# Query weights turned by VectorE in 32x32 blocks and gathered by small transfers, in place of identity products

## The chip, the cores and the metric

The kernel runs on one core of one Trainium2 chip. The time is device microseconds of the whole launch; the kernel before took 2062.61 us (median of three runs, 2061.29 to 2062.94). A profile of one more execution comes with it, and all durations below are from that execution. Engines are written as in the profile: PE is TensorE's matmuls, PEld its weight loads, DVE is VectorE, ACT is ScalarE, POOL is GpSimd, and SP (SPq) is SyncE, the queue that issues every transfer of this kernel.

## The reference: what is computed

Two stages follow each other over 4 batches of 12480 tokens with 128 channels.

1. Agent attention. 49 agents per batch attend to all keys and gather the values (`agent_v`, 49x128). Every query then attends to the 49 agents, and its softmax weights (49 numbers per token) mix `agent_v`.
2. A feed-forward layer over all 49920 tokens: `max(x @ w_in, 0)` squared, times `w_out`, with 2048 hidden channels.

```python
a2k = sm(agents, k)
agent_v = a2k @ v
q2a = sm(q, agents)
x = q2a @ agent_v
h = np.maximum(x @ w_in, 0.0)
out = h * h @ w_out
```

All inputs and outputs are float32.

## The kernel before

**Folding.** The kernel never forms `x`. It folds `agent_v @ w_in` into one table per batch (`aw_hi`, 128 rows by 2048 hidden channels), and multiplies the query weights of a token (49 numbers) with it directly. To keep float32 precision with fp32r operands, both factors are split into a high and a low part. The operand `w` therefore stacks 128 rows: rows 0 to 48 are the high parts of the 49 weights, rows 49 to 97 the low parts, and rows 98 to 127 a copy of rows 0 to 29, which meets the low parts of the table there. The 19 high rows that no longer fit (30 to 48) are copied four times into a second operand `x`, one copy at the start of each 32-row group, for a short product with K = 19.

**Tiling.** Tokens are handled in 52 blocks of 960 (`BLK`), 13 per batch. A block has two halves of 480 tokens (`G`), and each half passes through 16 chunks of 128 hidden channels. The main loop counts *slots* `k`: a slot is one pair of chunks of one half, so a block has 16 slots, 0 to 7 for the first half (j = 0) and 8 to 15 for the second. Two slots are issued together. For each such pair PE has four long products with `w` (`first`, into `h`), four short ones with `x`, and twelve products of the second layer (`second`, into `o`), which lag four slots behind. ACT takes `relu` and the square's high part, DVE the product `r*h` and half of the low parts, POOL the other half of the low parts (L372). The column `L337` in the profile is the helper `queued`, which issues all of these in one fixed order per engine.

**Query weights.** `queries(g)` prepares the weights of block g while block g-1 runs. It is a generator, and the main loop lets it go one step in slot 0 and one step in each slot from 2 on. The steps before the change: load `qt` (L285); eight tiles of 120 tokens times the 49 agents (L290, PSUM tile `psa`); the maximum and the subtraction on DVE (L293, L295); `exp` on ACT (L297); the sum, its reciprocal and the scaling of `e` (L300 to L303, the last on POOL); the split into `pp` (120 tokens by 8 tiles by 98), high part on ACT (L188) and low part on POOL (L190). Here tokens lie on partitions, while `w` needs the 49 agents on partitions. So for each half PE multiplies four tiles of `pp` by a 120x120 identity (L312), ACT copies the 98x480 result into `w` (L317), and SP issues one copy for rows 98 to 127 of `w` (L320) and four for `x` (L322). `w` and `x` have two buffers for each half.

**Background.** In the first three batches, another generator prepares the keys, values and tables of the next batch in the same slots (`background`: lines 141 to 277 of the profile). The last batch has no such work. Before the main loop a preamble loads the weights and does batch 0 and the first block's query weights.

**What sets the order.** `queued` chains the main work of PE, ACT and DVE by hand. Everything else is put into the engines' streams by a planner when the program is built: it plays the program on a timeline with costs of its own, and an instruction that stands earlier in the program goes first among those that are ready. On the chip each engine, and SP, then runs its stream strictly in that order. An instruction that waits holds up all that stands behind it on its engine.

Of the kernel before, what the change touches and what calls it, by code (L numbers as in the profile page):

```python
# [9 lines left out]
F32 = mybir.dt.float32  # L10
F32R = mybir.dt.float32r
# [6 lines left out]
P = 128  # L18
TP = 120
NT = 8  # L20
BLK = TP * NT
G = BLK // 2
# [16 lines left out]
def agent_attention_relu2(ctx: ExitStack, tc: tile.TileContext, qT, kT, v, agT, w_in, w_out, outT):  # L39
    nc = tc.nc  # L40
    C, NTOK = qT.shape
    _, B, NA = agT.shape
    N = NTOK // B
# [4 lines left out]
    K2 = 2 * NA  # L48
    SP = P - K2
    NL = NA - SP  # L50
    NQ = P // 32
    scale = 1.0 / math.sqrt(C)

    const = ctx.enter_context(tc.tile_pool(name="const", bufs=1))
# [3 lines left out]
    aw = ctx.enter_context(tc.tile_pool(name="aw", bufs=2))  # L58
    qp = ctx.enter_context(tc.tile_pool(name="qp", bufs=2))
# [8 lines left out]
    nc.gpsimd.memset(ones, 1.0)  # L68
    ident = const.tile([P, P], F32, name="ident")
    make_identity(nc, ident)  # L70
    identr = const.tile([TP, TP], F32R, name="identr")
    nc.scalar.copy(identr, ident[:TP, :TP])

    quad = const.tile([K2, 2, NA], F32, name="quad")
    nc.gpsimd.tensor_copy(quad, ident[:K2, :K2].rearrange("p (h a) -> p h a", h=2))
# [50 lines left out]
    last = {}  # L126
# [3 lines left out]
    def bank():  # L130
        if alone[0]:
            return ps_h.tile([P, 2, 512], F32, name="h")[:, 0, :]
        return ps_a.tile([P, 512], F32, name="psa")
# [51 lines left out]
    def halves(out, x, n, eng):  # L185

        w = x.shape[2]
        nc.scalar.copy(out[:, :, :w], x)  # L188
        yield
        last[eng] = eng.tensor_sub(out[:, :, n : n + w], x, out[:, :, :w].bitcast(F32))  # L190
# [52 lines left out]
    def tables(b):  # L243
        st = state[b]
        qd = quad.rearrange("p h a -> p (h a)")
        if "x" not in st:
            st["x"] = small.tile([K2, C + 1], F32, name="x")
            nc.vector.tensor_add(st["x"], st["av"][:, : C + 1], st["av"][:, C + 1 :])
        x = st["x"]
        yield  # L250
        pa = bank()
        nc.tensor.matmul(pa[:C, :K2], x[:, :C], qd, start=True, stop=True)
        nc.tensor.matmul(pa[:K2, K2 : K2 + 1], qd, x[:, C:], start=True, stop=True)
        yield
        av = small.tile([C, K2], F32, name="avT")
        nc.scalar.copy(av, pa[:C, :K2])
        rl = small.tile([K2, 1], F32, name="rl")
        nc.vector.tensor_scalar_add(rl, pa[:K2, K2 : K2 + 1], 1e-9)
        nc.vector.reciprocal(rl, rl)
        hi = st["hi"] = aw.tile([P, FF], F32R, name="aw_hi")  # L260
        ex = st["lo"] = aw.tile([P, NCH // NQ, P], F32R, name="aw_ex")
        for n in range(FF // 512):
            yield
            cs = slice(n * 512, (n + 1) * 512)
            pw = bank()
            nc.tensor.matmul(pw[:K2, :], av, win[:, cs], start=True, stop=True)  # L266
            yield
            last[nc.scalar] = nc.scalar.activation(hi[:K2, cs], pw[:K2, :], AF.Copy, scale=rl)
            lo = aw.tile([NA, 512], F32R, name="aw_lo", bufs=3)
            last[nc.vector] = nc.vector.scalar_tensor_tensor(  # L270
                out=lo, in0=pw[:NA, :], scalar=rl[:NA, :], in1=hi[:NA, cs].bitcast(F32),
                op0=ALU.mult, op1=ALU.subtract,
            )
            yield
            nc.sync.dma_start(hi[K2:, cs].bitcast(F32), lo[:SP, :].bitcast(F32))
            for t in range(NQ):
                nc.sync.dma_start(ex[t * 32 : t * 32 + NL, n, :].bitcast(F32), lo[SP:, t * P : (t + 1) * P].bitcast(F32))


    weights = {}  # L280

    def queries(g):
        b = g // NB
        qt = qp.tile([C, BLK], F32, name="qt", bufs=1)
        nc.sync.dma_start(qt, qT[:, g * BLK : (g + 1) * BLK])  # L285
        yield
        ps = bank()
        sv = ps[:TP, : NT * NA].rearrange("p (t a) -> p t a", a=NA)
        for t in range(NT):
            nc.tensor.matmul(sv[:, t, :], qt[:, t * TP : (t + 1) * TP], ag[:, b, :], start=True, stop=True)  # L290
        yield
        m = qp.tile([TP, NT, 1], F32, name="m", bufs=1)
        nc.vector.reduce_max(m, sv, axis=AX.X)  # L293
        e = qp.tile([TP, NT, NA], F32, name="e", bufs=1)
        nc.vector.tensor_sub(e, sv, m.broadcast_to([TP, NT, NA]))  # L295
        yield
        nc.scalar.activation(e, e, AF.Exp, scale=scale)  # L297
        yield
        z = qp.tile([TP, NT, 1], F32, name="z", bufs=1)
        nc.vector.reduce_sum(z, e, axis=AX.X)  # L300
        nc.vector.tensor_scalar_add(z, z, 1e-9)  # L301
        nc.vector.reciprocal(z, z)
        nc.gpsimd.tensor_mul(e, e, z.broadcast_to([TP, NT, NA]))  # L303
        yield
        pp = qp.tile([TP, NT, K2], F32R, name="pp", bufs=1)
        yield from halves(pp, e, NA, nc.gpsimd)
        weights[g] = []
        for j in range(2):
            yield
            pt = bank()  # L310
            for t in range(NT // 2):
                nc.tensor.matmul(  # L312
                    pt[:K2, t * TP : (t + 1) * TP], pp[:, j * (NT // 2) + t, :], identr, start=True, stop=True
                )
            w = qp.tile([P, G], F32R, name=f"w{j}", bufs=2)
            x = qp.tile([P, G], F32R, name=f"x{j}", bufs=2)
            nc.scalar.copy(w[:K2, :], pt[:K2, :G])  # L317
            weights[g].append((w, x))
            yield
            nc.sync.dma_start(w[K2:, :].bitcast(F32), w[:SP, :].bitcast(F32))  # L320
            for t in range(NQ):
                nc.sync.dma_start(x[t * 32 : t * 32 + NL, :].bitcast(F32), w[SP:NA, :].bitcast(F32))  # L322

    NP = NCH // 2
# [74 lines left out]
    def background(b):  # L401

        kt = load_keys(b, 0, kv, "kt")
        for i in range(NB):
            nxt = load_keys(b, i + 1, kv, "kt") if i + 1 < NB else load_values(b, 0, kv, "vt")
            yield from scores(b, i, kt)
            yield
            kt = nxt
        yield from maxima(b)
        yield  # L410
        vt = kt
        for i in range(NB):
            nxt = load_values(b, i + 1, kv, "vt") if i + 1 < NB else None
            yield from values(b, i, vt, nc.gpsimd)
            yield
            vt = nxt
        yield from tables(b)
# [24 lines left out]
    with tc.tile_pool(name="pre", bufs=PRE) as pre:  # L442
        for i in range(NB):
            kt = load_keys(0, i, pre, "ahead")
            run(scores(0, i, kt))
            warm(WARM1, ones, kt[:, :P])
        for n in range(WIN):
            load_w_in(dec, n)
        q0 = queries(0)
        next(q0)  # L450
        vts = []
        for i in range(min(PRE, NB)):
            vts.append(load_values(0, i, pre, "ahead"))
            if WIN + i < NW:
                load_w_in(dec, WIN + i)
        next(q0)
        with tc.high_priority():
            run(maxima(0))
        next(q0)
        for i in range(NB):  # L460
            whole_values(0, i, vts[i])
            if i + PRE < NB:
                vts.append(load_values(0, i + PRE, pre, "ahead"))
            if i >= QAT:
                next(q0, None)
        run(q0)
        with tc.high_priority():
            whole_sums(0)
            run(tables(0))
# [12 lines left out]
    for k in range(total + LAG):  # L482
        if k < total:
            g, c = divmod(k, SLOTS)
            b, i = divmod(g, NB)
            if i == 0 and c == 0 and b + 1 < B:
                todo = background(b + 1)
                done = 0
            goal = (i * SLOTS + c + 1) * STEPS / (SPREAD * NB * SLOTS)
            while done < goal and step(todo):  # L490
                done += 1
            if c == 0 and g + 1 < B * NB:
                ahead = queries(g + 1)
                step(ahead)
            if c >= 2:
                step(ahead)
        if k % 2 == 0:
            hs = first(k) if k < total else ()
            if hs:
                hidden(k, hs[0])  # L500
            for n in range(2):
                if k + n >= LAG:
                    second(k + n - LAG)
            copied_out()
            if hs:
                hidden(k + 1, hs[1])
# [31 lines left out]
```

## Time and profile before

| | |
|---|---|
| median of the runs | 2062.61 us |
| profiled execution | 2060.99 us |
| its span (first to last instruction) | 2059.2 us |
| mean granted clock of PE | 0.992 |
| busy share: PE, ACT, DVE, PEld, POOL | 99%, 87%, 82%, 77%, 62% |
| transfers issued by SP | 52 `qt`, 104 `out_T`, 104 `w`, 416 `x`, 104 loads of keys and values, and some 100 more |

The profile lists groups of instructions with count, busy time and mean duration, the idle time of an engine with what ended it, and a timeline of every engine. In a timeline row stand the start, the duration, the engine, the line of the kernel, and what is written from what. For `SPq` rows, the duration is the time in which SP issues a transfer, not the time in which the bytes move.

### The profile page before, as it was taken

How to read it: one execution, taken by the hardware profiler on the slowest of the kernel's cores; microseconds unless marked ns; L12 is line 12 of the kernel's file. 1: busy time of each engine (PE TensorE's matmuls, PEld its weight loads, DVE VectorE, ACT ScalarE, POOL GpSimd, SP SyncE). 2: the span in 40 equal slices, each digit the busy share in tenths (PEclk: the TensorE clock that was granted, in tenths of full speed). 3: DMA queues.
4: the chain of work that ended last, by engine and by line, in shares of the span. 5: the costliest groups of instructions: out<-in, count | busy, mean ns of one | idle time of the engine just before them, and what ended most of it. 6: DMA issues, size and time to landing. Idle time of an engine off the chain costs nothing.

```text
span 2059.2 us, 31857 instructions
## 1 busy us (share of the span) xinstructions
PE 2029.8 (99%) x11014; PEld 1589.8 (77%) x11014; DVE 1686.1 (82%) x1842; ACT 1782.3 (87%) x2100; POOL 1279.2 (62%) x1104
## 2 busy tenths in 40 slices
PE   9799999999999999999999999999999999999999
PEld 8588777777788777777778877777777777777777
DVE  5687888888887888888887788888888888888887
ACT  3478999989888899989888899998889898989897
POOL 3555787765544587776555467877555555656555
PEclk9799999999999999999999999999999999999999
DMA  9532122121122221221112212211111111111100
GB/s 288 160 92 76 59 72 74 53 77 41 45 81 65 62 72 54 72 71 57 55 54 69 68 42 61 74 58 49 42 50 36 45 36 46 37 41 36 38 23 20
DMA packets 55604, 131.36 MB, mean 64 GB/s; under 512 B 6660, under 2 KB 34388, under 8 KB 55444
## 3 DMA queue, kind: packets, MB, share of 16 engines
q1 hardware_dynamic: 55444, 129.33, 21.0%
q8 instruction: 88, 1.44, 0.3%
q14 instruction: 72, 0.59, 0.1%
HBM read 80.97 MB, written 25.56 MB: 52 GB/s over the span
## 4 chain that ended last, share of the span: by engine, by line
PE 53%; DVE 1%; issue 0%; ACT 0%
PE o L337 33%; PE h L337 16%; PE psa L290 2%; PE psa L155 1%; PE psa L312 1%; PE psa L235 1%; PE psa L266 0%; DVE h L337 0%; DVE gg L337 0%; DVE g_lo L337 0%; DVE z L301 0%; ACT r L337 0%; DVE ob L337 0%; ACT g_hi L337 0%; DVE av L241 0%
## 5 line engine op out<-in xcount | busy, mean ns | idle before, releaser
L372 POOL TENSOR_TENSOR g_lo<-gg,g_hi 128x480 fp32r<-128x480 f32 x832 | 999.2, 1222 | 685.7 <-DVE gg L337 489.1
L337 ACT ACTIVATE r<-h 128x960 f32<-128x960 f32 x832 | 800.9, 963 | 150.0 <-PE h L337 141.9
L337 ACT ACTIVATE g_hi<-r 128x960 fp32r<-128x960 f32 x832 | 837.7, 1007 | 34.1 <-POOL e L190 0.7
L337 DVE TENSOR_TENSOR h<-r,h 128x960 f32<-128x960 f32 x416 | 482.4, 1160 | 160.2 <-ACT r L337 157.8
L337 DVE TENSOR_TENSOR gg<-r,h 128x960 f32<-128x960 f32 x416 | 477.8, 1149 | 81.9 <-ACT r L337 81.0
L337 PE MATMUL o<-g_hi,wo_hi 128*128 128x480 f32 x1664 | 543.0, 408 | 0.0
L337 DVE TENSOR_TENSOR g_lo<-h,g_hi 128x960 fp32r<-128x960 f32 x416 | 480.8, 1156 | 45.2 <-ACT g_hi L337 8.1
L337 PE MATMUL o<-g_hi,wo_lo 128*128 128x480 f32 x1664 | 498.7, 381 | 0.0
L337 PE MATMUL o<-g_lo,wo_hi 128*128 128x480 f32 x1664 | 497.7, 380 | 0.0
L337 PE MATMUL h<-w,aw_hi 128*128 128x480 f32 x1664 | 483.3, 398 | 9.7 <-DVE gg L337 8.1
L337 PEld LDWEIGHTS o<-g_hi,wo_hi 128*128 128x128 f32 x1664 | 280.8, 188 | 118.8 <-issue 70.1
L337 PEld LDWEIGHTS o<-g_hi,wo_lo 128*128 128x128 f32 x1664 | 313.4, 188 | 51.3
L337 PEld LDWEIGHTS o<-g_lo,wo_hi 128*128 128x128 f32 x1664 | 313.0, 188 | 50.9
L337 PEld LDWEIGHTS h<-w,aw_hi 128*128 128x128 f32 x1664 | 289.0, 190 | 56.9 <-DVE gg L337 17.5
L337 PE MATMUL h<-x,aw_ex 19*128 19x480 f32 x1664 | 205.4, 481 | 0.1
L337 PEld LDWEIGHTS h<-x,aw_ex 19*128 19x128 f32 x1664 | 80.5, 182 | 140.7 <-issue 139.7
L290 PEld LDWEIGHTS psa<-ag,qt 128*120 128x120 f32 x816 | 102.2, 187 | 7.8 <-issue 1.4
L337 DVE COPY ob<-o 128x480 f32<-128x480 f32 x104 | 68.3, 656 | 39.8 <-PE o L337 38.3
L290 PE MATMUL psa<-ag,qt 128*120 128x49 f32 x816 | 98.1, 264 | 0.0
L190 POOL TENSOR_TENSOR vs<-vt,vs 120x1024 fp32r<-120x1024 f32 x39 | 86.3, 2213 | 16.7 <-ACT vs L188 16.4
L155 PEld LDWEIGHTS psa<-ag,kt 128*120 128x120 f32 x624 | 74.7, 185 | 4.8 <-DVE mx L163 0.6
L155 PE MATMUL psa<-ag,kt 128*120 128x49 f32 x624 | 71.9, 262 | 0.2 <-DVE mx L163 0.2
(109 smaller groups left out, 1026.6 us busy)
## 6 DMA issues: line engine op xcount, KB each, us to landing
qt<-in_qT SPq DMA_DIRECT2D x52, 480.0 KB
out_T<-ob SPq DMA_DIRECT2D x104, 240.0 KB
kt<-in_kT SPq DMA_DIRECT2D x39, 480.0 KB
vt<-in_v SPq DMA_DIRECT2D x39, 480.0 KB
x<-w SPq DMA_DIRECT2D x416, 35.6 KB
ahead<-in_kT SPq DMA_DIRECT2D x13, 480.0 KB
ahead<-in_v SPq DMA_DIRECT2D x13, 480.0 KB
w<-w SPq DMA_DIRECT2D x104, 56.2 KB
```

What stands on the lines that cost most here:

```text
L155: nc.tensor.matmul(sv[:, t, :], kt[:, t * TP : (t + 1) * TP], ag[:, b, :], start=True, stop=True)
L190: last[eng] = eng.tensor_sub(out[:, :, n : n + w], x, out[:, :, :w].bitcast(F32))
L235: nc.tensor.matmul(pv[:K2, :W], e[:, t, :], vs[:, t, :], start=(t == 0), stop=(t == NT - 1))
L290: nc.tensor.matmul(sv[:, t, :], qt[:, t * TP : (t + 1) * TP], ag[:, b, :], start=True, stop=True)
L312: nc.tensor.matmul(pt[:K2, t * TP : (t + 1) * TP], pp[:, j * (NT // 2) + t, :], identr, start=True, stop=True)
L337: ins = issue(*args, **kw)
L372: nc.gpsimd.tensor_sub(lo[:, n, :], gg[:, n, :], hi[:, n, :].bitcast(F32))
```

## The change

Tokens and agents change places in another way. The scaled weights `e` now live in a tile `qe` of 128 partitions by 8 tiles by 64 columns, of which 120 by 8 by 49 are written and the rest stays zero. One DVE instruction turns it in blocks of 32x32: afterwards partition 32r+i holds agent i (block a = 0) or agent 32+i (a = 1) of the tokens 32r to 32r+31 of each tile. ACT then copies the turned tile into a high part `turned_hi`, and POOL subtracts to leave the low part in `turned`.

Since a block stays in its group of 32 partitions, the rows of `w` have to be gathered. For each of the high and the low part, each half j, each a (32 or 17 agents) and each of the four partition groups r (32, 32, 32 and 24 tokens) SP issues one transfer: 32 transfers per block. A row of such a transfer is 128 numbers in one run, or for r = 3 four runs of 24 numbers. The four copies for `x` and the one for rows 98 to 127 follow as before. The generator has 14 steps now: high part j = 0, high part j = 1, low part j = 0, low part j = 1, and then the copies of each half.

The columns of `w` come in another order by this. The host reorders the columns of `qT` within each half, so that the output stands as before. The identity `identr`, the tile `pp` and the products and copies that used them go; `aw_lo` has two buffers instead of three.

```diff
-    identr = const.tile([TP, TP], F32R, name="identr")
-    nc.scalar.copy(identr, ident[:TP, :TP])
+    qe = const.tile([P, NT, 64], F32, name="qe")
+    nc.gpsimd.memset(qe, 0.0)
...
-            lo = aw.tile([NA, 512], F32R, name="aw_lo", bufs=3)
+            lo = aw.tile([NA, 512], F32R, name="aw_lo")
...
-        e = qp.tile([TP, NT, NA], F32, name="e", bufs=1)
+        e = qe[:TP, :, :NA]
...
-        pp = qp.tile([TP, NT, K2], F32R, name="pp", bufs=1)
-        yield from halves(pp, e, NA, nc.gpsimd)
-        weights[g] = []
-        for j in range(2):
-            yield
-            pt = bank()
-            for t in range(NT // 2):
-                nc.tensor.matmul(
-                    pt[:K2, t * TP : (t + 1) * TP], pp[:, j * (NT // 2) + t, :], identr, start=True, stop=True
-                )
-            w = qp.tile([P, G], F32R, name=f"w{j}", bufs=2)
-            x = qp.tile([P, G], F32R, name=f"x{j}", bufs=2)
-            nc.scalar.copy(w[:K2, :], pt[:K2, :G])
-            weights[g].append((w, x))
+        lo = qp.tile([P, 2, NT, 32], F32R, name="turned", bufs=1)
+        nc.vector.transpose(
+            lo.bitcast(F32).rearrange("p a t i -> p t a i"), qe.rearrange("p t (a i) -> p t a i", i=32)
+        )
+        yield
+        hi = qp.tile([P, 2, NT, 32], F32R, name="turned_hi", bufs=1)
+        nc.scalar.copy(hi, lo.bitcast(F32))
+        yield
+        last[nc.gpsimd] = nc.gpsimd.tensor_sub(lo, lo.bitcast(F32), hi.bitcast(F32))
+        weights[g] = [
+            (qp.tile([P, G], F32R, name=f"w{j}", bufs=2), qp.tile([P, G], F32R, name=f"x{j}", bufs=2)) for j in range(2)
+        ]
+        for y, at in ((hi, 0), (lo, NA)):
+            for j, (w, _) in enumerate(weights[g]):
+                yield
+                ts = slice(j * NT // 2, (j + 1) * NT // 2)
+                for a, rows in enumerate((32, NA - 32)):
+                    for r in range(NQ):
+                        n = min(32, TP - r * 32)
+                        cs = slice(r * 32 * NT // 2, (r * 32 + n) * NT // 2)
+                        to = w[at + a * 32 : at + a * 32 + rows, cs].bitcast(F32)
+                        nc.sync.dma_start(
+                            to.rearrange("p (t i) -> p t i", i=n), y[r * 32 : r * 32 + rows, a, ts, :n].bitcast(F32)
+                        )
+        for j, (w, x) in enumerate(weights[g]):
             yield
             nc.sync.dma_start(w[K2:, :].bitcast(F32), w[:SP, :].bitcast(F32))
             for t in range(NQ):
                 nc.sync.dma_start(x[t * 32 : t * 32 + NL, :].bitcast(F32), w[SP:NA, :].bitcast(F32))
```

More of the change, by code (lines that the diff above doesn't have):

```diff
@@ L517 @@
     B, N, C = q.shape
+    halves = q.reshape(-1, G, C)
+    edge = TP // 32 * 32
+    turned = halves[:, : edge * NT // 2].reshape(-1, edge // 32, NT // 2, 32, C).transpose(0, 2, 1, 3, 4)
+    turned = np.concatenate(
+        [turned.reshape(-1, NT // 2, edge, C), halves[:, edge * NT // 2 :].reshape(-1, NT // 2, TP - edge, C)], axis=2
+    )
     given = {
-        "qT": np.ascontiguousarray(q.reshape(B * N, C).T),
+        "qT": np.ascontiguousarray(turned.reshape(B * N, C).T),
         "kT": np.ascontiguousarray(k.reshape(B, N // BLK, TP, NT, C).transpose(4, 0, 1, 3, 2)).reshape(C, B * N),
```

## The prediction

> **What bounds the kernel now.** I read the page's totals first, then PE's timeline over one block of the last batch, where no background work is mixed in.
>
> ```profile
> span 2059.2 us, 31857 instructions
> ...
> PE 2029.8 (99%) x11014; PEld 1589.8 (77%) x11014; DVE 1686.1 (82%) x1842; ACT 1782.3 (87%) x2100; POOL 1279.2 (62%) x1104
> ...
> PE 53%; DVE 1%; issue 0%; ACT 0%
> ```
>
> PE is busy for 99% of the span, and the chain that ended last is PE nearly alone, as far back as it was followed. Whatever PE no longer has to do is gained, as long as its operands come in time.
>
> ```profile
> 1913.18 1.36 PE L290 MATMUL psa<-ag,qt 128*120 128x49 f32 x12
> ...
> 1948.51 1.36 PE L290 MATMUL psa<-ag,qt 128*120 128x49 f32 x12
> ...
> 1966.67 0.60 PE L337 MATMUL h<-w,aw_hi 128*128 128x480 f32 x2
> 1967.11 0.48 PE L312 MATMUL psa<-identr,pp 120*98 120x120 f32 x4
> 1967.43 0.65 PE L337 MATMUL h<-w,aw_hi 128*128 128x480 f32 x2
> 1968.01 0.49 PE L337 MATMUL h<-x,aw_ex 19*128 19x480 f32 x4
> ...
> 1971.16 0.48 PE L312 MATMUL psa<-identr,pp 120*98 120x120 f32 x4
> ...
> 1972.49 0.49 PE L337 MATMUL h<-x,aw_ex 19*128 19x480 f32 x4
> ...
> 1975.64 1.04 PE L337 MATMUL h<-w,aw_hi 128*128 128x480 f32 x4
> 1976.62 0.49 PE L337 MATMUL h<-x,aw_ex 19*128 19x480 f32 x4
> ...
> 1979.76 1.04 PE L337 MATMUL h<-w,aw_hi 128*128 128x480 f32 x4
> 1980.73 0.50 PE L337 MATMUL h<-x,aw_ex 19*128 19x480 f32 x4
> ```
>
> From the scores of one block's queries to those of the next lie 1948.51 - 1913.18 = 35.33 us. The scores at 1948.51 belong to the block whose first products are those at 1979.76 (`w`) and 1980.73 (`x`): its first half must have its weights by then, 32.2 us after its scores.
>
> **What is removed.** From the first `w` product to the `x` products PE takes 0.98 us undisturbed (1975.64 to 1976.62), 1.34 us with the first group of identity products in between (1966.67 to 1968.01), and 1.33 us behind the second (1971.16 to 1972.49). That is 0.36 + 0.35 = 0.71 us of PE per block, and 51 blocks do it inside the main loop: **-36.2 us**. It is all that the change can win, since no other engine bounds the loop.
>
> **What DVE, ACT and POOL get.**
>
> ```profile
> L295 DVE TENSOR_TENSOR e<-psa,m 120x392 f32<-120x392 f32 x51 | 28.7, 563 | 1.3
> L337 DVE TENSOR_TENSOR h<-r,h 128x960 f32<-128x960 f32 x416 | 482.4, 1160 | 160.2 <-ACT r L337 157.8
> L190 POOL TENSOR_TENSOR pp<-e,pp 120x392 fp32r<-120x392 f32 x52 | 50.3, 968 | 6.8 <-ACT pp L188 6.8
> L317 ACT CAST w<-psa 98x480 fp32r<-98x480 f32 x102 | 55.7, 546 | 2.8 <-PE psa L312 1.6 <-PE h L337 0.3
> ```
> ```profile
> L188 ACT CAST pp<-e x52: 507/513/521, 47.7 to 1962.7; 120x392 fp32r<-120x392 f32 x52
> ```
> ```profile
> 1944.30:1979.70 35.40, 35.40 (x186) 27.39 (x185) 30.20 (x32) 32.06 (x37) 20.93 (x18) 1.00 0.08 27
> ```
>
> The last row is one block: its length, then the busy time of PE, PEld, DVE, ACT and POOL. A turn on DVE is not in the trace. By its 512 elements per partition it lies between the rows for 392 (0.56 us) and 960 (1.16 us), and I take 0.7 us; DVE has 35.40 - 30.20 = 5.2 us free per block, which covers either end, and without that cover it would cost 36 us in all. ACT gains: one copy of 512 columns (some 0.6 us) for one of 0.513 and two of 0.546. POOL's subtraction grows from 0.968 to some 1.3 us, with 14 us free. None of the three moves the end by its work.
>
> **What SP gets: this decides.** It issues 32 more transfers per block, each from SBUF to SBUF.
>
> ```profile
> L320 SPq DMA_DIRECT2D w<-w x104: 835/856/968, 61.6 to 1981.6; - x104
> L322 SPq DMA_DIRECT2D x<-w x416: 564/565/1526, 63.6 to 1984.4; - x139
> ```
> ```profile
> L382 SPq DMA_DIRECT2D out_T<-ob x104: 332/344/447, 122.9 to 2055.9; - x104
> ```
> ```profile
> L94 SPq DMA_DIRECT2D raw<-in_w_in x8: 327/351/558, 10.2 to 42.9; - x8
> L94 SPq DMA_DIRECT2D raw<-in_w_out x8: 367/379/404, 55.4 to 77.7; - x8
> ```
> ```profile
> 1933.10 0.86 SPq L320 DMA_DIRECT2D w<-w  x1
> 1934.06 2.48 SPq L322 DMA_DIRECT2D x<-w  x4
> ```
> ```profile
> 1935.20:1941.60 6.40, 6.40 (x36) 4.75 (x34) 4.83 (x6) 5.71 (x7) 3.93 (x4) 1.00 0.06 22
> ```
>
> Median issue times: a copy of 30 rows inside SBUF 0.856 us, one of 19 rows 0.565 us, a store of 128 rows to HBM 0.344 us. Four in a row take 2.48 us, so 0.07 us lies between two. Of the 32 new transfers 16 have 32 rows and 16 have 17. For 17 rows I take 0.54 us (nearest row 0.565; the two SBUF rows as a line give (0.856 - 0.565) / 11 = 26.5 ns a row and 0.51). For 32 rows the bounds are 0.34 (the store, 128 rows) and 0.91 (the line); I take 0.88, since the copy of 30 rows is nearest in kind and size. A quarter of each kind has rows in four runs. A load whose rows come in two runs (`in_w_out`) is issued in 0.379 us against 0.351 in one: I charge nothing for runs; the upper bound is 26.5 ns for each further run, 4 x (96 + 51) x 0.0265 = 15.6 us per block. Together 16 x 0.88 + 16 x 0.54 + 32 x 0.07 = **25.0 us** of SP per block, 16.3 at the lower bound, 40.6 at the upper.
>
> Now the path of one block's weights, from its scores at 1948.51.
>
> ```profile
> 1960.98 0.84 POOL L303 TENSOR_TENSOR e<-e,z 120x392 f32<-120x392 f32 x1
> ```
>
> The scaled weights are there at 1961.8. The turn (0.7 us, behind a DVE instruction in hand) and ACT's copy (0.6 us, also behind one) end at about 1965. POOL's low part comes some 2 us later, and SP needs it only after its first 16 transfers, so it costs nothing; without these 12 us of cover it would cost its 2 us. SP then issues 32 transfers until 1990.0. Behind them in its queue stand an `out_T` store (0.41), the `w` copy (0.95) and the four `x` copies. Those for 1934.06 moved until 1941.6: the window holds 6.4 us x 22 GB/s = 141 KB, four times 35.6 KB, and its share of 0.06 is one of 16 DMA engines. So the last `x` copy lands 7.5 us after the first is issued, at 1998.9. Without identity products PE would want it at 1980.73 - 0.71 = 1980.0. **It is 18.8 us late.** The second half's weights follow by 3.6 us of issue and are wanted half a block later. Each `out_T` store waits up to 20 us in the queue, but `ob` has two buffers for two stores in 35 us; loads of keys, values and `qt` are issued a step ahead. I count nothing for them.
>
> Is every block late? PE's order is the planner's, and the trace shows what that does where it expects transfers to be late.
>
> ```profile
> 84.75 1.22 PE L337 MATMUL h<-x,aw_ex 19*128 19x480 f32 x3
> 85.90 1.88 PE L155 MATMUL psa<-ag,kt 128*120 128x49 f32 x16
> 87.70 0.48 PE L337 MATMUL h<-x,aw_ex 19*128 19x480 f32 x1
> ```
>
> Three `x` products ran, then sixteen score products of the background, then the fourth `x` product, whose table row the last of four transfers brings: PE's stream was filled with ready work in front of a late operand. The query scores are such work too (their `qt` is loaded early, and nothing chains them to the main products). So in front of a late block the planner should place the scores of the block after it, some 19 us early. That block is then in time, and its own successor, with its scores at the usual place, is late again. **Every second block late by 18.8 us** is what I take: 25.5 x 18.8 = +479 us. In the first three batches the blocks are longer, and the path grows with them about as the deadline does; I use the same figure. In the preamble the path from 47.7 ends near 47.7 + 0.6 + 25.0 + 0.95 + 7.5 = 81.8, ahead of the first `x` products at 84.75, so it adds nothing.
>
> The sum against the profiled execution: 2059.2 - 36.2 + 479.4 = 2502.4, and 1.8 us around the span (2060.99 - 2059.2), so **2504 us**. The profiled execution is 1.6 us below the median of the runs, which the forecast ignores.
>
> **Rivals.**
>
> *Hidden after all, faster.* SP's work per block in the last batch would be 25.0 + 2 x (0.95 + 2.55) for `w` and `x` + 2 x 0.41 + 0.42 for stores and `qt` = 33.2 us, of the 34.6 us that PE needs: it fits, if barely. If the planner places the scores at least 18.8 us earlier in every block, or the transfers are cheap enough to make up half of that, all weights come in time, and the time is 2059.2 - 36.2 + 1.8 = **2025 us**. For it speaks that PE's order is free there; against it, that the planner moves scores only where it sees PE idle, and then PE was idle. The Trainium skill (DMA: Bandwidth & Descriptors, Issuing engines are not separate DMA queues) says that the time for a sequencer to initiate a DMA is usually small relative to the DMA itself; by that rule this rival is the outcome, 2025 us. The trace does not bear it out for these shapes: 17 rows of 512 B are 8.7 KB, 0.4 us at the 22 GB/s of the window above, and their issue takes 0.54 us.
>
> *The planner does not see it.* If its costs for a transfer are so low that the weights look timely, all scores stay at their place, and each of 51 blocks is late: 2059.2 - 36.2 + 51 x 18.8 + 1.8 = **2984 us**. For it speaks the order of the trace, where scores stand in the same slot in block after block; against it the rows at 84.75.
>
> *Copies of 32 rows cost no more than a store.* 0.34 us in place of 0.88 takes 16 x 0.54 = 8.6 us off the path; 10.2 us late in every second block gives +260 us, **2285 us**. The store has four times the rows and is issued in 0.344 us, so rows alone don't set the cost; but no copy inside SBUF was issued in under 0.564 us.
>
> *Each run is charged.* 15.6 us more per block: SP's 48.8 us exceed PE's time, and 34.4 us late in every second block gives +877 us, **2902 us**. Only the two-run load speaks on it, against. With every block late it would be 3779 us.
>
> *No change.* Almost everything is hidden, and waits in SP's queue eat the 0.7 us per block: **2061 us**.
>
> **How the numbers follow.** Every second block late 35%; all blocks late 15%; cheap copies 15%; runs charged 12%, and with every block late 3%; hidden 15%; no change 5%. The likeliest gives 2504 us. From 2050 to 3000 us the range leaves out the hidden case and 3779, 18% together. A measurement of this kernel tells about 0.2% from no change: faster 15%, same 5%, slower 80%.
>
> **What would show it.** In the profile after: no `identr` products, and 0.98 us from `w` to `x` products throughout; SP rows of 0.88 and 0.54 us for the new transfers, and SP busy for some 25 us per block in one train; PE idle in front of the first `w` or `x` product of a block, released by a transfer, with query scores just ahead of that wait. Wrong I am if PE stays at 99% (then the scores were moved enough, or the copies are cheap: their rows tell which), if the wait stands in front of another engine (DVE held by the turn, whose target has a single buffer and must wait for the transfers of the block before, with all of `r*h` queued behind it), or if bytes in flight and not SP's issue are what is late.

## The result, and the profile after

The changed kernel takes **2523.35 us** (median of four runs, 2520.44 to 2524.33) against 2061.95 us of the kernel before, timed beside it (2061.27 to 2062.94): a ratio of 1.2235, 95% interval 1.2214 to 1.2256. The forecast was 2504 us, with a range of 2050 to 3000. The size is close, but the way to it was another one, as the runs below show.

The page after: span, engines' totals, the chain that ended last, then two groups of PE whose idle time grew.

```profile
span 2520.9 us, 32970 instructions
...
PE 2198.9 (87%) x10598; PEld 1683.5 (67%) x10598; DVE 1731.9 (69%) x1894; ACT 1758.1 (70%) x1995; POOL 1294.7 (51%) x1105
...
PE 6%; SPq 3%; DMA 1%; DVE 1%; issue 0%; ACT 0%; POOL 0%; DVEq 0%
...
L347 PE MATMUL h<-x,aw_ex 19*128 19x480 f32 x1664 | 278.1, 509 | 98.0 <-DMA x<-w 97.8
...
L290 PE MATMUL psa<-ag,qt 128*120 128x49 f32 x816 | 123.5, 310 | 108.9 <-DMA qt<-in_qT 108.9
```

PE was busy for 99% of the span and is now at 87%, and transfers and SP stand in the chain. PE is idle for 2520.9 - 2198.9 = 322.0 us. What it waits for, from the view of waits (total, times, longest):

```profile
PE h L347 <- DMA x<-w: 111.4, 115, 6.7
PE psa L290 <- DMA qt<-in_qT: 108.9, 17, 9.8
PE h L347 <- DVE turned L306: 19.5, 7, 7.0
PE psa L155 <- DMA kt<-in_kT: 13.4, 4, 5.7
```

Two waits make up 220 us: the products at the start of a block for the copies in `x`, and the query scores for the load of `qt`. Here is what SP does around one such wait (timeline; the second number is the time SP spends on the issues of the row):

```profile
1131.21 10.40 SPq L326 DMA_DIRECT2D w<-turned_hi  x16
...
1157.00 3.06 SPq L333 DMA_DIRECT2D x<-w  x4
1160.18 8.46 SPq L326 DMA_DIRECT2D w<-turned_hi  x8
...
1178.61 10.38 SPq L326 DMA_DIRECT2D w<-turned  x16
...
1193.99 2.46 SPq L333 DMA_DIRECT2D x<-w  x4
1196.49 0.59 SPq L285 DMA_DIRECT2D qt<-in_qT  x1
...
1224.32 1.85 SPq L326 DMA_DIRECT2D w<-turned_hi  x3
```

Two blocks' transfers stand back to back, from 1131 to 1196. Only then is `qt` issued. PE's timeline of the same place:

```profile
1208.71 3.44 PE L290 MATMUL psa<-ag,qt 128*120 128x49 f32 x16 [6.49 <-DMA qt<-in_qT]
...
1237.67 1.57 PE L290 MATMUL psa<-ag,qt 128*120 128x49 f32 x14
```

The load that was issued at 1196.49 lets PE go at 1208.71, 12 us later. The packets that the DMA engines moved, which the trace keeps one by one, show why. The load has 128 packets of 3840 bytes. 120 of them are done by 1199.9; then packets of 1920 bytes, as the copies into `x` have, move one after another until 1207.0 (beside them move loads that were issued later); the last eight packets of the load start at 1207.04, and the last ends at 1208.22. The maximum, `exp`, the sum and the turn follow, and the next transfer goes out at 1224.32. For 28 us SP has no weights to move, and then it again has two blocks' worth at once. The transfers and this chain stand one after the other where they should overlap.

Now the wait for `x`, again in PE's timeline:

```profile
2262.31 1.10 PE L347 MATMUL h<-w,aw_hi 128*128 128x480 f32 x4 [2.67 <-DVE turned L306]
2264.42 0.76 PE L347 MATMUL h<-x,aw_ex 19*128 19x480 f32 x1 [1.01 <-DMA x<-w]
2265.94 0.76 PE L347 MATMUL h<-x,aw_ex 19*128 19x480 f32 x1 [0.76 <-DMA x<-w]
2267.62 0.76 PE L347 MATMUL h<-x,aw_ex 19*128 19x480 f32 x1 [0.92 <-DMA x<-w]
2269.08 0.76 PE L347 MATMUL h<-x,aw_ex 19*128 19x480 f32 x1 [0.70 <-DMA x<-w]
...
2270.74 1.00 PE L347 MATMUL o<-g_hi,wo_lo 128*128 128x480 f32 x2
...
2276.44 0.59 PE L347 MATMUL o<-g_hi,wo_lo 128*128 128x480 f32 x2
```

SP issues the four copies within 2.5 us, but they land 1.5 us apart, one by one: 35.6 KB in 1.5 us is 24 GB/s. And behind the wait the same pair of products takes 1.00 us, and 0.59 us six microseconds later. The windows of that place (PE busy, PEld, DVE, ACT, POOL, granted clock, DMA share, GB/s) say why:

```profile
2240.00:2259.60 19.60, 19.60 (x104) 15.20 (x102) 16.50 (x19) 17.24 (x19) 11.47 (x11) 1.00 0.12 30
2259.60:2269.10 9.50, 3.44 (x9) 1.54 (x8) 4.68 (x6) 4.05 (x6) 3.41 (x3) 0.73 0.11 32
2269.78:2274.50 4.72, 4.72 (x13) 3.98 (x13) 1.26 (x2) 1.97 (x2) 2.66 (x3) 0.53 0.11 33
2275.90:2280.00 4.10, 4.10 (x25) 3.13 (x21) 2.39 (x4) 3.85 (x4) 1.61 (x2) 1.00 0.09 20
```

The granted clock falls during the wait and stays near 0.5 for some time after PE has work again. The Trainium skill (TensorE: Matmul & The Clock Gate, HAM oscillation — how this bites in real kernels) gives as its rule that PE must have no idle gap longer than about 3.4 us, or the gate goes back to half clock. The trace agrees on the fall, with 0.53 behind a stretch of 9.5 us in which PE worked for 3.44, but not on the length: no single wait there is longer than 2.67 us.

Counted from the `w` products (32 to a block), the time went here. A block starts with its first `w` product.

```
stretch                    before     after    difference
start of block 0            83.71     91.44       +7.7
blocks 0 and 1              93.50    117.20      +23.7
blocks 2 to 38, each        38.35     47.53    37 x +9.18 = +339.6
blocks 39 to 50, each       35.05     41.98    12 x +6.93 =  +83.1
block 51 to the end         42.40     49.94       +7.5
```

In blocks 4 to 38 long and short ones often alternate, for instance 40.50 us for block 22 and 55.51 for block 23.

### The profile page after: what moved, and what is told of

It reads as the page before. It is cut to its first block, busy times and chain, and to the rows that moved or that the text cites. A ratio compares the mean times of both kernels' runs of the same rounds, so it can differ in the third digit from the quotient of the medians.

```text
span 2520.9 us, 32970 instructions
## 1 busy us (share of the span) xinstructions
PE 2198.9 (87%) x10598; PEld 1683.5 (67%) x10598; DVE 1731.9 (69%) x1894; ACT 1758.1 (70%) x1995; POOL 1294.7 (51%) x1105
## 5 line engine op out<-in xcount | busy, mean ns | idle before, releaser
L347 PE MATMUL o<-g_hi,wo_hi 128*128 128x480 f32 x1664 | 573.2, 427 | 2.6 <-ACT turned_hi L311 2.6
L347 PE MATMUL o<-g_hi,wo_lo 128*128 128x480 f32 x1664 | 523.6, 397 | 0.0
L347 PEld LDWEIGHTS h<-w,aw_hi 128*128 128x128 f32 x1664 | 316.5, 201 | 143.1 <-issue 39.1
L347 PEld LDWEIGHTS o<-g_hi,wo_hi 128*128 128x128 f32 x1664 | 299.4, 201 | 130.6 <-issue 55.9
L347 PEld LDWEIGHTS o<-g_hi,wo_lo 128*128 128x128 f32 x1664 | 334.3, 201 | 53.6
L347 PE MATMUL h<-x,aw_ex 19*128 19x480 f32 x1664 | 278.1, 509 | 98.0 <-DMA x<-w 97.8
L347 PEld LDWEIGHTS h<-x,aw_ex 19*128 19x128 f32 x1664 | 107.2, 192 | 284.6 <-issue 141.9
L290 PE MATMUL psa<-ag,qt 128*120 128x49 f32 x816 | 123.5, 310 | 108.9 <-DMA qt<-in_qT 108.9
L290 PEld LDWEIGHTS psa<-ag,qt 128*120 128x120 f32 x816 | 123.2, 230 | 122.0 <-DMA qt<-in_qT 116.2
L293 DVE TENSOR_REDUCE m<-psa 120x8 f32<-120x392 f32 x51 | 28.6, 561 | 155.6 <-PE psa L290 154.9
## 6 DMA issues: line engine op xcount, KB each, us to landing
x<-w SPq DMA_DIRECT2D x416, 35.6 KB
```

What stands on the lines that cost most here:

```text
L347: ins = issue(*args, **kw)
```

## The experiments

Three theories. **B** is the recorded one: SP's issue time on the path from a block's scores to its products. **A**: SP's queue order, because the load of `qt` has one buffer and waits behind two blocks' transfers. **C**: the copies into `x` move through one DMA engine one behind the other, and hold up the products that need them and the loads behind them. Three edits of the changed kernel, alone and together, tell them apart; all eight combinations were timed. Where an edit changes the number of transfers or of buffers, the planner lays out the order anew, so it acts through the order too.

**Two buffers for `qt`** (theory A). To make room, the loads of the weights have three buffers and `rest` one.

```diff
-        qt = qp.tile([C, BLK], F32, name="qt", bufs=1)
+        qt = qp.tile([C, BLK], F32, name="qt", bufs=2)
```

> The changed kernel, with two buffers for qt, so that a block's query load needs no longer wait for the scores of the block before and can stand ahead of the transfers on SP (room for it comes from raw with 3 and rest with 1 buffer, which only the preamble uses). Theory A (the load of qt stands in SP's queue behind the transfers of two blocks, and its landing and the score chain, some 28 us, stand in series with them every second block): PE's waits for qt, 109 us in the profile after, vanish, the serial stretch of 28 us per two blocks goes, and with it 26 x 20 to 26 x 28 us: 1800 to 2000 us by the sum, which PE's own work cuts off at some 2030 to 2150 us. Theory B (as predicted: 25 us of issue on each block's own path make every second block late, whenever qt comes): the time stays within 2% of 2523 us.

Measured: 2265.28 us, ratio 1.0989 (1.0967 to 1.1011), granted clock 0.941 against 0.892. The waits show where the gain came from and what is late next:

```profile
DVE turned L306 <- DMA w<-turned: 66.2, 31, 5.3
...
PE o L347 <- ACT turned_hi L311: 40.3, 24, 4.4
...
PE psa L290 <- DMA qt<-in_qT: 27.6, 5, 9.7
```

Without a single transfer less, 258 us are gone, though fewer than theory A said (2030 to 2150 us). PE's waits for `x` fell with those for `qt`, from 111.4 to 6.3 us. So SP's issue time by itself was not the cause (against B); that `qt` stood behind it in the queue was a large part. What is left at `turned` is the turn on DVE, which waits for the block before to leave its only buffer, and ACT's copy behind it, with the main work queued after both.

**One transfer for both halves.** `w` and `x` become one tile with both halves; 20 transfers and five copies per block are left of 32 and ten.

```diff
-            (qp.tile([P, G], F32R, name=f"w{j}", bufs=2), qp.tile([P, G], F32R, name=f"x{j}", bufs=2)) for j in range(2)
+        w = qp.tile([P, 2, G], F32R, name="w", bufs=2)
+        x = qp.tile([P, 2, G], F32R, name="x", bufs=2)
...
+                        if n == 32:
+                            nc.sync.dma_start(to, src.rearrange("p (j t) i -> p j (t i)", j=2))
```

> The changed kernel, with one tile for both halves of w and of x, so that one transfer serves both halves (for 24 tokens, where a third dimension would come in, still one for each half): 20 transfers instead of 32, one w copy instead of two, four x copies instead of eight. 25 issues per block instead of 42, with the same bytes. Theory A: the train of a block falls from some 30 us to 18, the two-block cycle from 93 us to about 2 x 18 + 28 = 64, less than PE's 75: 2030 to 2150 us. Theory B: 12 x 0.65 us less on the path, 18.8 - 7.8 - 3.4 = 7.6 us late in every second block: 2059 - 36 + 25.5 x 7.6 = 2217 us. If bytes in flight on one DMA engine decide (x copies, 6.4 us each half), nothing is gained: 2500 us.

Measured: 2189.91 us, ratio 1.0627 (1.0611 to 1.0644), clock 0.955, which neither theory A (2030 to 2150 us) nor B (2217 us) gave. **Both together:**

> Both edits, merged transfers and two qt buffers. Theory A: all hidden, PE busy at 98 to 99% and its clock back near 0.99: 2020 to 2040 us, faster than the kernel before by up to the 36 us of identity products. Theory B: about 2217 us, as without the second qt buffer.

Measured: 2169.48 us, ratio 1.0521 (1.0504 to 1.0539). 258 and 333 us apart, 354 us together: the edits take away the same waits. The time is far from A's 2020 to 2040 us: what remained was not explained by A. From the waits and the timeline of PE with both edits:

```profile
PE psa L155 <- DMA kt<-in_kT: 43.4, 5, 11.5
PE h L266 <- ACT avT L256: 22.4, 1, 22.4
```
```profile
664.57 3.01 PE L155 MATMUL psa<-ag,kt 128*120 128x49 f32 x14 [7.18 <-DMA kt<-in_kT]
```

Loads of keys land late at a batch's change, just behind the copies into `x`. That led to theory C.

**Copies of 20 rows in place of 19.** The added row is never read by a product. 19 is prime; the Trainium skill (DMA: Bandwidth & Descriptors, Why a DMA increments its semaphore by 16 and not by 1) says that a copy issued by SP is spread over the largest number of engines up to 16 that divides its rows: one engine for 19 rows, ten for 20. The trace agrees: in the kernel before, the 76 packets of four copies of 19 rows (from 1935.33 to 1941.89) never move two at once, and in the same kernel with copies of 20 rows (the control below) up to ten move at once and the 20 packets of a copy start within 0.22 us.

```diff
-                nc.sync.dma_start(x[t * 32 : t * 32 + NL, :].bitcast(F32), w[SP:NA, :].bitcast(F32))
+                nc.sync.dma_start(x[t * 32 : t * 32 + NL + 1, :].bitcast(F32), w[SP : NA + 1, :].bitcast(F32))
```

> The changed kernel with one edit: each copy into the x tile takes 20 rows instead of 19 (the extra row is never read by a product). Theory C: in the changed kernel the copies of 19 rows go through one DMA engine one behind the other, 1.5 us each, so the products on x wait for them (111.4 us over 115 waits) and whatever load stands behind them on that engine lands late (the 17 waits for qt's load). If so, copies of 20 rows end the waits of PE for x (below 30 us) and shorten qt's landing from 9 to 12 us to 3 to 5 us; about 80 us of the x waits, 60 to 90 us of the qt waits and a part of the half clock that follows a stall go: 2250 to 2400 us. Theory A (only the place of qt's load in SP's queue behind the transfers of two blocks counts, not the engine): the x waits turn into waits for something else and the qt waits stay at 9 us and more: 2450 to 2520 us. Theory B (the recorded prediction: SP's issue time itself delays the products): nothing is issued less, so 2500 to 2530 us.

Measured: 2242.76 us, ratio 1.0882 (1.0866 to 1.0899), clock 0.950. 281 us for one row more (theory C said 2250 to 2400), though SP issues each such copy more slowly (the row of the changed kernel, then that of this one; shortest, median and longest in ns):

```profile
L333 SPq DMA_DIRECT2D x<-w x416: 561/571/1703, 85.9 to 2475.2; - x139
```
```profile
L333 SPq DMA_DIRECT2D x<-w x416: 717/718/1038, 87.6 to 2200.7; - x139
```

The waits of PE:

```profile
PE psa L290 <- DMA qt<-in_qT: 25.0, 15, 3.7
PE h L347 <- DMA w<-w: 21.6, 6, 7.0
...
PE h L347 <- DMA x<-w: 15.6, 24, 5.5
```

111.4 became 15.6 and 108.9 became 25.0: `qt`, which has one buffer and the same place in the queue, lands soon once the copies ahead of it are spread. Another buffer starts the load earlier, spread copies let it land sooner; either takes most of the same wait away. Theory A's 2450 us is refuted. The order is not quite the same here (28 of SP's 2541 issues and 458 of PE's 10598 products stand elsewhere); the next pairs leave that out.

**Copies of 20 rows with the merged transfers**, with one and with two buffers for `qt`.

> Transfers for both halves at once and copies of 20 rows, but one buffer for qt. Theory A (qt's load stands behind the transfers in SP's queue): with one buffer its issue waits for the scores before it and then behind a shorter train; its waits return in part: 2090 to 2150 us. Theory C alone (only the one engine): 2060 to 2080 us.

Measured: **2059.79 us**, ratio 0.9990 (0.9981 to 0.9999).

> Transfers for both halves at once, two buffers for qt and copies of 20 rows into x. Against the 2169.48 us of the same kernel with copies of 19 rows. Theory C: key loads at a batch's change land late because of the x copies on one DMA engine (five waits of 11.5 us there), so these waits shrink below 4 us each, and the granted clock rises from 0.958 to 0.98 or more: 2050 to 2110 us; with everything hidden but the preamble's 15 us longer start, 2040 us. Theory A (the place in SP's queue alone): the waits at the batch's change stay, 2150 to 2170 us.

Measured: 2067.04 us, ratio 1.0029 (1.0016 to 1.0041). These two give the sharpest comparison of all. Each has, instruction for instruction, the same order on PE, DVE, ACT, POOL and SP as its partner with copies of 19 rows (1657 issues of SP alike). The row alone is worth 2189.91 - 2059.79 = 130 us and 2169.48 - 2067.04 = 102 us. With it, the second buffer of `qt` has no use: it costs 7 us, and the loss is in blocks 0 to 4 (227.2 against 217.1 us). That the weight loads gave up a buffer for it may be the reason; no run shows it. The waits of the kernel at 2059.79 us:

```profile
PE h L348 <- DVE gg L348: 15.4, 42, 1.7
PE h L266 <- ACT avT L256: 11.3, 1, 11.3
PE h L216 <- DVE e L211: 9.4, 1, 9.4
```

No transfer is left among the long ones.

**Copies of 20 rows and two buffers, transfers not merged** (theory B once more: 42 issues per block instead of 25).

> Copies of 20 rows into x and two buffers for qt, with the 42 small transfers per block left as they are. Theory B (SP's issue time delays the products even when no load waits behind it): the transfers of a block take about 21 us of SP in a block of 36 us and stand in order before the next loads, so most of the 175 us between 2242.76 and 2067.04 stays, 2180 to 2240 us. Theory C (what cost time was the single engine of the copies and the late qt): with both gone the number of issues hardly counts and the time is 2065 to 2110 us.

Measured: 2137.12 us, ratio 1.0352 (1.0325 to 1.0380). Between the two: against 2067.04 us the number of issues is worth 70 us here, not the 113 us or more of theory B and not the 43 us or less of theory C. (With one buffer for `qt` it is 183 us, 2242.76 against 2059.79.) Its partner with copies of 19 rows, 2265.28 us, has the same order on every engine, so the row is worth 128 us in this pair. Where the issues act:

```profile
DVE turned L306 <- DMA w<-turned: 50.5, 35, 3.8
...
PE o L347 <- ACT turned_hi L311: 34.0, 26, 3.5
```

The longer train keeps `turned` and `turned_hi` occupied; the turn and ACT's copy wait for it, and what PE needs stands behind them. So SP's issue time does act, through buffers and engines in order, and not on the path that the prediction drew.

All combinations in one table, in us:

```
                          32+10 issues    merged, 20+5 issues
19 rows, one qt buffer      2523.35            2189.91
19 rows, two qt buffers     2265.28            2169.48
20 rows, one qt buffer      2242.76            2059.79
20 rows, two qt buffers     2137.12            2067.04
```

**The control:** the kernel before with copies of 20 rows.

> Control: the kernel before with copies of 20 rows into x and nothing else. Its PE waits for a DMA hardly at all, so by every theory it takes the same time, 2050 to 2064 us.

Measured: 2061.52 us, ratio 1.0003 (0.9994 to 1.0013). Faster copies are worth nothing there, since nothing waited for the slow ones.

**The price of the identity products**, tested by itself: the kernel before with each of them issued twice.

```diff
-                nc.tensor.matmul(
-                    pt[:K2, t * TP : (t + 1) * TP], pp[:, j * (NT // 2) + t, :], identr, start=True, stop=True
-                )
+                for _ in range(2):
+                    nc.tensor.matmul(
+                        pt[:K2, t * TP : (t + 1) * TP], pp[:, j * (NT // 2) + t, :], identr, start=True, stop=True
+                    )
```

> The kernel before, with each identity product issued twice into the same place. It measures the term that the change removes. If these products cost PE 0.71 us per block, as the timeline says: 2062 + 36 = 2098 us (2092 to 2104). If they are hidden in PE's waits: 2062 us; if the bank they hold is what costs, up to 2130 us.

Measured: 2103.69 us, ratio 1.0202 (1.0187 to 1.0217), that is 41.5 us more (39 to 45), 0.8 us per block. As an added cost the term of 36 us is about right.

**Two attempts to get below the kernel before.** In the kernel at 2059.79 us PE waits 11.3 us for `avT` in the preamble, because ACT's copy stands behind a load of `w_out` that SP issues after the first block's transfers. First, the first four loads of `w_out` are no longer put ahead of the tables (`EARLY` 0 for 4; with two `qt` buffers):

> Transfers for both halves at once, two buffers for qt, copies of 20 rows, and the first four loads of w_out no longer ahead of the agents' tables on ScalarE (EARLY 0 in place of 4). The kernel without the last edit stands at 2067.04 us; its trace has one wait of 12.65 us of TensorE for avT, because ScalarE's copy stands behind a w_out load that SP issues only after the first block's transfers, and block 0 runs at a granted clock of 0.79. If that is the rest of the loss, the first product comes some 8 us sooner and the time is 2048 to 2060 us, below the kernel before. If w_out, now later, holds up the first second-layer products instead, 2064 to 2075 us.

Measured: 2072.83 us, ratio 1.0054 (1.0041 to 1.0067). Then, with one `qt` buffer, these loads issued from ACT's queue:

```diff
-        nc.sync.dma_start(flat if len(src.shape) == 2 else ...
+        queue.dma_start(flat if len(src.shape) == 2 else ...
```

> Transfers for both halves at once and copies of 20 rows, with the first four loads of w_out issued from ScalarE's queue and not from SP's. Without the last edit the time is 2059.79 us and its trace shows TensorE waiting 11.33 us for avT: ScalarE's copy stands behind a w_out load that SP issues at 81.4 us, after all transfers of the first block. If that load is the rest of the loss, the wait goes below 2 us, the first product comes at 82 to 84 us and not at 91.7, and the time is 2046 to 2054 us (ratio 0.992 to 0.996). If the last x copies (issued up to 81.3 us) or the tables' copies behind them take its place, as with EARLY 0, 2056 to 2066 us.

Measured: 2062.80 us, ratio 1.0007 (0.9996 to 1.0019). Neither falls below the kernel before. The wait for `avT` is gone, and another one stands in its place, a row of the first and a row of the second kernel:

```profile
86.71 1.14 PE L348 MATMUL h<-w,aw_hi 128*128 128x480 f32 x2 [11.06 <-DMA aw_hi<-aw_lo]
```
```profile
93.95 1.14 PE L349 MATMUL h<-w,aw_hi 128*128 128x480 f32 x2 [10.21 <-DMA aw_hi<-aw_lo]
```

The table's rows come by transfers too, and SP issues them behind the same train. In both, what was taken out of the queue left the next thing in it late by about as much. The control, the kernel before with the same loads on ACT's queue:

> Control: the kernel before with the same four loads of w_out issued from ScalarE's queue. There they were issued from 55 us on and nothing waited long for them (TensorE's copy avT came 0.76 us late), so the time is that of the kernel before, 2058 to 2066 us; if it falls by as much as the other kernel, the gain does not belong to the change.

Measured: 2061.09 us, ratio 1.0000 (0.9991 to 1.0009).

So the best version with the change is level with the kernel without it.

## Why the prediction was right, and where it was wrong

**The sign and the size** came out, 2504 against 2523 us. In blocks 2 to 38 it forecast 18.8 - 2 x 0.71 = 17.4 us more for each pair of blocks, and 2 x 9.18 = 18.4 us were measured. This nearness is luck and no support for the steps: several of them fell, and their errors made up for each other.

**The step that failed first: whose scores they are.** The path was measured against 32.2 us, because "The scores at 1948.51 belong to the block whose first products are those at 1979.76". They do not belong to it. From the views of the tiles `qt` and `w` of the kernel before (shortest, median and longest in ns, then first and last start):

```profile
L290 PE MATMUL psa<-ag,qt x816: 203/268/435, 93.8 to 1950.5; 128*120 128x49 f32 x164
```
```profile
L337 PE MATMUL h<-w,aw_hi x1664: 372/382/784, 83.7 to 2046.3; 128*128 128x480 f32 x185
```

The last scores of the program start at 1950.5, and `w` products follow for 95 us, which is more than two blocks. Counted from the front, the scores at 1948.51 belong to block 51, which starts at 2016.82: the deadline was 68.3 us away, and a path of 50.4 us met it. One look at the last scores would have shown this. In the first three batches the lead is 30 to 78 us, counted in the same way. By its own sum the prediction should then have forecast the last batch hidden, yet it lost 83 us there; and blocks 21 to 28, which had a lead of 51 to 78 us, lost 9.9 us each, no less than the others. The lateness comes from elsewhere.

**What came true of the pattern.** In blocks 17 to 23 of the changed kernel the scores stand 41 and 62 us ahead of their block by turns, and every wait of an `x` product for its copy stands before the first four `x` products of a block, as forecast. But these waits come to 98 us in all and to at most 7.3 us in one block, not to 18.8 us in every second one.

**The step that stands in its place** is a sentence that cost two things at nothing: "loads of keys, values and `qt` are issued a step ahead. I count nothing for them." The load of `qt` was issued behind two blocks' transfers and landed 12 us later, behind copies that go one by one. The prediction had seen those copies, four in 7.5 us on one of 16 engines, and charged them to the path alone, not to the loads that share the engine. The time lost in every second block comes from the same place: the transfers of two blocks back to back, then 28 us of load, scores and turn with nothing to move.

**SP's price** was set too high. From the view of the tile `w`, after:

```profile
L326 SPq DMA_DIRECT2D w<-turned_hi x832: 507/593/2197, 56.4 to 2455.5; - x167
L326 SPq DMA_DIRECT2D w<-turned x832: 507/596/1982, 74.6 to 2467.9; - x167
```

16 transfers take 10.38 us undisturbed, so 20.8 us per block against the 25.0 forecast. In the single records 32 rows take 0.58 us, 17 rows 0.56 to 0.65, and either of them in four runs 0.64 to 0.66. So the number of rows did not set the price, as the 0.88 us assumed, and the bound of 15.6 us for runs is refuted. (The upper bound of 40.6 us for SP was also added up with 0.88 and not with 0.91 us; with 0.91 it is 41.0.)

**A term that was missing: the clock.** The kernel at 2059.79 us has the same 10598 instructions on PE, and its page says:

```profile
PE 1999.2 (97%) x10598; PEld 1550.0 (75%) x10598; DVE 1716.7 (83%) x1894; ACT 1757.0 (85%) x1995; POOL 1298.2 (63%) x1105
```

Of the 2520.9 - 2058.0 = 462.9 us between the two spans, 2198.9 - 1999.2 = 199.7 us are the same work done more slowly, and 263.2 us are idle time. Between these two kernels each microsecond of waiting came with three quarters of another one of slower work. The prediction counted waits alone; that it reached the sum all the same is because its waits were too long: 479 us, where the idle time of PE grew by 322.0 - 29.4 = 292.6 (29.4 is 2059.2 - 2029.8, before).

**DVE, ACT and POOL** came out as forecast: 0.704 us for the turn (0.7), 0.609 for ACT's copy (0.6), 1.290 for POOL's subtraction (1.3).

**The gain of 36 us** came in PE's work, but not in the time, so that the rival *hidden after all* was too low: with no wait for a transfer left in the main loop the time is 2059.79 and not 2025 us. The windows of blocks 5 to 50 show it, first the kernel before, then that at 2059.79 us (columns as above):

```profile
293.92:2016.82 1722.90, 1718.49 (x9188) 1336.24 (x9187) 1435.06 (x1514) 1546.78 (x1796) 1093.60 (x926) 1.00 0.18 54
```
```profile
308.83:2016.32 1707.49, 1685.12 (x8756) 1293.49 (x8754) 1456.16 (x1546) 1518.41 (x1688) 1091.62 (x911) 1.00 0.23 63
```

PE works 33.4 us less in 46 blocks, 0.73 us per block where 0.71 was forecast. But it is idle for 22.4 us instead of 4.4, so the blocks are shorter by only 0.33 us each. Of these 18.0 us more, 8.2 are waits for `gg` and 6.7 for `g_lo`, both of DVE. DVE's and PE's timeline of that kernel shows one such wait:

```profile
1680.51 0.71 DVE L306 STREAM_TRANSPOSE turned<-qe 128x512 f32<-128x512 f32 x1 [1.22 <-DMA w<-turned]
...
1689.03 1.09 DVE L348 TENSOR_TENSOR gg<-r,h 128x960 f32<-128x960 f32 x1
```
```profile
1690.18 0.70 PE L348 MATMUL h<-w,aw_hi 128*128 128x480 f32 x2 [0.36 <-DVE gg L348]
```

The turn waits 1.22 us for its buffer and takes 0.71, and ten microseconds later PE waits 0.36 us for `gg`. So the 5.2 us that DVE has free per block, which were to cover the turn, did not keep PE from waiting for DVE. The prediction named this place under what would prove it wrong, but not as a cost of the hidden case. That the turn's wait for its buffer is what puts DVE behind, and that a second buffer of `turned` would bring the time back, is argued and wasn't tried. The rest of the gain is lost ahead of block 5: the first product comes 8.0 us later, since the preamble, which "adds nothing", is where loads and tables stand behind the first train, and blocks 0 to 4 take 6.9 us more.

**The other rivals**: *each run is charged* (2902 us) is refuted by the issue times above and *the planner does not see it* (2984 us) by the leads of 41 and 62 us and the short blocks between the long ones; of *copies of 32 rows cost no more than a store* (2285 us) half came true, 0.58 us between its 0.34 and the 0.88 taken, but the time did not follow the issue.

## What to carry to other kernels

In this kernel small transfers cost less by their number (70 us, once nothing else was late) than by where they stood: in a queue that runs in order, ask of each load behind them how late it now starts, and of each one-buffer tile who waits for it to be read. Before a path is compared with a deadline, count which block an instruction belongs to, from the first or the last of its kind. And look at the number of rows of a copy: one more took 102 to 281 us off this kernel, and nothing off the kernel before, where no engine waited for these copies.

## What the runs showed of the hardware that was not expected

- A copy of 20 rows lands so much sooner than one of 19 that 111.4 us of waits become 15.6, though its issue takes 0.718 us instead of 0.571. In three pairs of kernels with the same order of all instructions the row was worth 130, 128 and 102 us. The packets show the difference: one at a time with 19 rows, up to ten at once with 20. A load issued behind such copies is late as a whole, because in the load shown above the last eight of 128 packets start 7 us after the others are done.
- The issue time of a copy inside SBUF hardly depends on its rows: 0.58 us for 32 and 0.56 us and more for 17, yet 0.856 us for the 30 rows of `w<-w`. What sets it the runs leave open.
- Behind a stretch of 9.5 us in which PE was mostly idle, its granted clock stayed near 0.5 for about five microseconds of full work. No single wait in that stretch was longer than 2.67 us. Against the kernel at 2059.79 us, whose mean granted clock is 0.986 and not 0.892, the same products of PE took 199.7 us longer, beside 263.2 us more idle time.
